# Twenty weight pieces converted early and parked in DRAM, four PSUM banks with a lag of three pairs, and a polynomial kept in PSUM

## The chip, the cores and the metric

The kernel runs on one core of a Trainium2 chip. The metric is the device time of one execution in microseconds (us); three runs of the kernel before the change gave 1054.34, 1056.89 and 1063.83 us, a median of 1056.89 us. The engines named below are PE (matrix multiply), DVE (vector), ACT (scalar functions), POOL (general purpose), SP (it only issues DMAs here), and PEld, the loading of weights into PE beside the multiplications.

## What is computed

Three stages follow one another on 4 batches of 576 tokens (2304 tokens in all).

```python
# stage 1: causal attention, 8 heads of width 64, plus a linear memory term
a = softmax(causal(q @ k.T / 8));  local = a @ v
mem_out = (phi(q) @ M_prev) / (phi(q) @ z_prev + 1e-6)     # phi(x) = elu(x) + 1
x = g * mem_out + (1 - g) * local                          # g = sigmoid(beta), per head
# stage 2, "first layer" (moe): 2304 x 512 -> 2048 -> 512
h = x @ moe_w_in;  x = (max(h, 0) + log1p(exp(-abs(h)))) @ moe_w_out
# stage 3, "second layer" (moe2): 2304 x 512 -> 2048 -> 512
h = x @ moe2_w_in
P = a0 + a1*h + a2*h**2 + a3*h**3;  Q = 1 + abs(b0)*abs(h) + abs(b1)*h**2
out = (P / (Q + 1e-6)) @ moe2_w_out
```

The four weight matrices arrive as 64-bit floats. The kernel has no 64-bit arithmetic, so each weight has to be put together as a 32-bit float from its two 32-bit halves by shifts and masks; below this is called converting.

## The kernel before, in words

**Pieces.** Each weight matrix is cut into 16 pieces of 128 partitions x 512 weights: 512 KB as it arrives, 256 KB once converted. `load_piece` issues the DMA. A piece is converted in one of two ways: `bits` takes three DVE instructions, `bits_abs` two on DVE, two on ACT and a multiplication on POOL. The tables `SIGN` and `SIGN2` say which piece takes which way. After that the pieces of moe_w_in, moe_w_out and moe2_w_in are scaled and split into a high and a low 16-bit float (`w_split`); the pieces of moe2_w_out become a high and a low 32-bit part (tiles w2oh and w2ol).

**First layer.** Tokens come in 12 groups (j = 0 to 11), each with 8 pairs of hidden rows, so that 96 pairs Q are worked off in order. `g1(Q)` multiplies a pair into PSUM bank 2 or 3 (`hf`), ACT takes Relu, Abs, Exp and Ln, DVE adds and subtracts, and the result goes into one of four buffers GH. `g2(Q)` multiplies GH into the accumulators in banks 0 and 1. PE gets g1(Q) and then g2(Q - LAG), with LAG = 2. Each of g1 and g2 is 24 matmuls with 160, 192 or 256 columns. Attention of later batches runs between the pairs and uses banks 4 to 7. The two first groups work in 32-bit floats and have fewer matmuls.

**Second layer.** The tokens are 6 blocks of 384 and the hidden rows 16 slices of 128, which gives 96 steps F. `h1(F)` is 12 matmuls of 384 columns into one of the banks 2 to 5 (`hp`, F modulo 4). ACT forms |h| and h squared, Ln and Exp (the reciprocal of Q); DVE forms the polynomial in six instructions; ACT rounds the result to its high part and POOL subtracts (tile `gr`). `h2_(F - 3)` is 9 matmuls of 512 columns into the accumulators, from `gr` and w2oh or w2ol. PE gets h1(F), then h2_(F - 3).

**What sets the order.** The program is first written down as a list of operations with keys. A planner, `Program.order`, then simulates the engines with a cost for each operation (`cost`) and a table of latencies, and on each engine takes the ready operation with the lowest key; `P.key` serves all engines and `P.pkey` serves PE. Some operations can go to one of two or three engines (`P.flex`), and the planner chooses. `P.emit` (L374, in the changed kernel L392) issues everything in this fixed order, so that nearly every row of the profile has that one line. All DMAs go through SP's queue, in order: a DMA that has to wait holds those behind it.

**The pieces of the second layer.** They have keys K0 = 1000 and up, after all of attention. They are loaded into two buffers (RAW2) in the space that attention has left, converted, and put in place: 16 pieces of moe2_w_in first (W2I), then 16 of moe2_w_out (W2O). The scale of moe2_w_in needs the largest weight of all 16 pieces, so that no split starts before the last of them is converted.

## Time and profile before

| | |
|---|---|
| median of three runs | 1056.89 us (1054.34 to 1063.83) |
| the profiled execution: time, span | 1058.07 us, 1056.1 us |
| mean granted clock of PE (share of full speed) | 0.976 |
| busy: PE, DVE, ACT, POOL | 984.7, 925.8, 837.8, 375.3 us |

The span runs from the first to the last instruction; the execution's own time is 2.0 us longer. Attention and the first layer fill the time to about 535 us; from there to about 650 us the rest of the first layer runs beside the conversion of the second layer's weights; then comes the second layer alone. The groups of rows below are cut from the profile's views: busy time by stretch, instructions in order of time, instructions grouped by form, and DMA issues. In a row of a view in order of time the bracket at the end holds the idle time before the instruction and what ended it.

### The profile page before, as it was taken

To read this page: it belongs to the slowest core of one execution; us is meant where nothing else is said; L and a number is where in the kernel's file an instruction comes from. 1 tells how busy PE (TensorE), PEld (TensorE's weight loads), DVE (VectorE), ACT (ScalarE), POOL (GpSimd) and SP (SyncE) were. 2 spreads that over 40 slices of the span, in tenths; PEclk is the share of its full clock that TensorE was granted. 3 is DMA by queue.
4 is the path that set the end of the run, shared out by engine and by line. 5 is a ranking of instruction groups with operands and counts; after the bars stand their busy time and mean duration, and the time that the engine had idled before them with its cause. 6 is when DMAs were issued, how large, how long until landed. Compare 5 with 4: busy or idle time off the path is not lost.

```text
span 1056.1 us, 22659 instructions
## 1 busy us (share of the span) xinstructions
PE 984.7 (93%) x8252; PEld 774.7 (73%) x8252; DVE 925.8 (88%) x2151; ACT 837.8 (79%) x1948; POOL 375.3 (36%) x427
## 2 busy tenths in 40 slices
PE   7779999999989999899898897998999999999998
PEld 6556777877778888788797896665766666666666
DVE  7999679988988997877768799999999999999896
ACT  5887978779889998777878777777778778687875
POOL 4323467852342422231033344333223223232222
PEclk9979999999999999989999999998999999999999
DMA  9986367577899977755755533010101000000000
GB/s 257 313 213 170 74 131 141 102 138 143 151 144 167 168 151 125 141 112 101 119 157 177 182 100 127 20 41 1 60 1 36 25 31 31 1 31 1 31 1 30
DMA packets 242975, 109.48 MB, mean 104 GB/s; under 512 B 218416, under 2 KB 224560, under 8 KB 242864
## 3 DMA queue, kind: packets, MB, share of 16 engines
q1 hardware_dynamic: 242864, 108.04, 45.6%
q8 instruction: 64, 1.05, 0.4%
q14 instruction: 47, 0.39, 0.1%
HBM read 59.25 MB, written 9.44 MB: 65 GB/s over the span
## 4 chain that ended last, share of the span: by engine, by line
PE 45%; DVE 14%; ACT 9%; DMA 6%; issue 3%; POOL 1%; SPq 1%; ACTq 0%; DVEq 0%; POOLq 0%
PE bank L374 45%; DVE arena L374 9%; ACT arena L374 5%; ACT bank L374 3%; DMA arena<-arena 2%; DMA arena<-in_moe_w_in_dram 2%; DVE bank L374 2%; DVE tiny L374 1%; SPq L374 1%; DMA arena<-in_moe_w_out_dram 0%; DMA arena<-x2d 0%; ACT a L374 0%; POOL arena L374 0%; DMA arena<-in_v_dram 0%; DVE a L374 0%
## 5 line engine op out<-in xcount | busy, mean ns | idle before, releaser
L374 PE MATMUL bank<-arena,w 128*128 128x160 f16 (+3 forms) x4288 | 422.4, 259 | 25.1 <-DVE arena L374 24.0
L374 PE MATMUL bank<-arena 128*128 128x384 f16 (+11 forms) x2852 | 356.6, 299 | 28.4 <-DVE arena L374 12.3
L374 ACT ACTIVATE arena<-bank,tiny 128x384 f32<-128x384 f32 (+8 forms) x538 | 300.0, 588 | 91.3 <-PE bank L374 81.2
L374 PEld LDWEIGHTS <-w 128*128 128x128 f16 x3840 | 298.9, 99 | 41.4 <-issue 32.4
L374 PEld LDWEIGHTS <-arena 128*128 128x128 f16 (+1 forms) x2464 | 159.9, 104 | 130.8 <-issue 58.1
L374 PE MATMUL bank<-w2oh,gr 128*128 128x512 f32 x576 | 206.2, 416 | 0.0
L374 POOL TENSOR_TENSOR gr<-arena,gr 128x384 fp32r<-128x384 f32 x94 | 102.0, 1085 | 262.2 <-ACT gr L374 240.5
L374 DVE SCALAR_TENSOR_TENSOR arena<-arena,tiny 128x384 f32<-128x384 f32 (+6 forms) x182 | 147.5, 823 | 11.2 <-ACT arena L374 9.5
L374 ACT ACTIVATE arena<-arena 128x384 f32<-128x384 f32 (+4 forms) x213 | 123.3, 580 | 13.4 <-DMA arena<-in_moe_w_in_dram 4.6
L374 PEld LDWEIGHTS bank<-w2oh,gr 128*128 128x128 f32 x576 | 109.5, 190 | 27.1 <-POOL gr L374 0.4
L374 DVE SCALAR_TENSOR_TENSOR arena<-arena 128x384 f32<-128x384 f32 (+3 forms) x168 | 117.8, 702 | 5.7 <-ACT arena L374 4.8
L374 POOL TENSOR_TENSOR arena<-arena 128x512 f32<-128x512 f32 (+6 forms) x68 | 66.2, 981 | 144.3 <-ACT arena L374 69.3
L374 ACT ACTIVATE bank<-bank,tiny 128x384 f32<-128x384 f32 (+4 forms) x192 | 102.5, 538 | 17.1 <-DVE tiny L374 16.1
L374 PE MATMUL bank<-w2ol,gr 128*128 128x512 f32 x288 | 114.3, 397 | 0.7 <-POOL w2ol L374 0.7
L374 ACT ACTIVATE bank<-bank 128x320 f32<-128x320 f32 (+2 forms) x208 | 103.5, 497 | 2.3
L374 ACT ACTIVATE arena<-bank 128x320 f16<-128x320 f32 (+5 forms) x148 | 72.1, 495 | 31.0 <-DVE bank L374 19.5
L374 PEld LDWEIGHTS bank<-arena,w 128*128 128x128 f32 x448 | 82.8, 190 | 14.0 <-issue 1.7
L374 DVE SCALAR_TENSOR_TENSOR arena<-bank,tiny,arena 128x384 f16<-128x384 f32 (+3 forms) x112 | 64.6, 592 | 19.1 <-ACT arena L374 17.2
L374 POOL TENSOR_SCALAR arena<-arena,tiny 128x640 f16<-128x640 f32 (+8 forms) x70 | 55.1, 793 | 61.8 <-DVE tiny L374 29.7
L374 ACT ACTIVATE arena<-arena,qe 128x384 f32<-128x384 f32 x96 | 58.9, 613 | 20.5 <-DVE arena L374 20.0
L374 DVE CUSTOM_DVE_ANT_0 bank<-bank,mask,tiny 128x384 f32<-128x384 f32 (+4 forms) x112 | 67.0, 609 | 5.8 <-PE bank L374 3.1
L374 DVE SCALAR_TENSOR_TENSOR arena<-arena,bb 128x384 f32<-128x384 f32 x96 | 67.0, 698 | 3.1 <-ACT arena L374 3.1
(108 smaller groups left out, 1115.2 us busy)
## 6 DMA issues: line engine op xcount, KB each, us to landing
arena<-in_moe_w_out_dram SPq DMA_DIRECT2D x32, 512.0 KB, 3.9
arena<-in_moe_w_in_dram SPq DMA_DIRECT2D x24, 512.0 KB, 4.9
arena<-in_k_dram SPq DMA_DIRECT2D x44, 128.0 KB, 3.6
arena<-in_v_dram SPq DMA_DIRECT2D x44, 128.0 KB, 2.9
arena<-arena SPq DMA_DIRECT2D x32, 160.0 KB, 3.0
arena<-x2d SPq DMA_DIRECT2D x6, 768.0 KB, 4.2
out_dram<-arena SPq DMA_DIRECT2D x18, 256.0 KB, 2.1
w<-in_moe_w_in_dram SPq DMA_DIRECT2D x8, 512.0 KB, 9.1
```

What stands on the lines that cost most here:

```text
L374: fn(**{k: (v.fn() if isinstance(v, Lazy) else v) for k, v in kw.items()})
```

## The change

- **Early pieces.** After pass 3 (the pass with all tokens of batch 3) `w2_early` takes all 16 pieces of moe2_w_in and 4 of moe2_w_out. It has keys from 2000 up, behind everything else. It loads each piece into the upper part of XA or XF, converts it into tile a1, and writes the 256 KB to a DRAM buffer `w2d`. Two of three pieces take the way of three DVE instructions (`SIGN3`). Behind attention the 20 pieces are then read from `w2d` to where they were converted to before.
- **Banks and lag.** LAG goes from 2 to 3, and pairs from Q = 80 on use banks 2 to 5 in turn for `hf`.
- **Polynomial in PSUM.** In `h1` two DVE instructions write their result back into the bank `hp` (before: into SBUF buffer l1), and a third reads it from there. The bank is thus in use up to the last of the six DVE instructions; before it was free after the third (the row that names `aa`).
- **Planner.** It now keeps a bank from being planned for two engines at once (`held`), and counts a pointer operand named `scale` in DVE's cost. The order of the whole program is made anew with this.

```diff
--- before.py
+++ after.py
@@ -22,7 +22,9 @@
 NT = B * S
 TB2 = 384
 NPAIR = DF // 256
-LAG = 2
+LAG = 3
+
+QLATE = 80
 PORT = 0.8
 EARLY = lambda load, u, consts, batch: (
     (lambda: load(u[0], 0, 1), lambda: load(u[1], 0, 1)),
...
@@ -48,6 +50,11 @@
 SIGN = ((1, 0), (0,))
 SIGN2 = ((1,), (0, 0, 1))
 LO_POOL = False
+
+NST = (16, 4)
+EARLY2 = {3: (0, 20)}
+KEY_ST = 2000
+SIGN3 = (0, 0, 1)
 BACKLOG = 4000.0
 NRAW = 6
 NGH = 4
...
@@ -138,7 +145,7 @@
         if name == "reciprocal":
             return 67 + 6.2 * n
         one = name in ("tensor_scalar", "tensor_copy", "memset") and not psum
-        aps = sum(is_ap(kw.get(k)) for k in ("scalar", "scalar1", "scalar2"))
+        aps = sum(is_ap(kw.get(k)) for k in ("scalar", "scalar1", "scalar2", "scale"))
         return (77 if name == "tensor_tensor_reduce" else 67) + (0.52 if one else 1.042) * n + 62 * aps
     if eng == "ACT":
         more = is_ap(kw.get("scale")) + is_ap(kw.get("bias")) + ("accum_out" in kw)
...
@@ -229,6 +236,9 @@
 
     def _deps(self, op, rd, wr):
         preds = set()
+        for v in rd + wr:
+            if is_psum(v):
+                op.banks.add(v.tensor.name)
         for v in rd:
             self._touch(span(v), op, False, preds)
         for v in wr:
...
@@ -288,6 +298,8 @@
         port = {"DVE": 0.0, "POOL": 0.0}
 
         now = dict.fromkeys(engines, 0.0)
+
+        held = {}
 
         def release(o):
             o.cand = {"BULK"} if o.bulk and "SP" in o.alts else set(o.alts)
...
@@ -326,6 +338,10 @@
                 continue
             k, i = heapq.heappop(ready[e])
             o = self.ops[i]
+            t = max((x + LATENCY[f][e] for b in o.banks for f, x in held.get(b, {}).items() if f != e), default=0.0)
+            if t > s:
+                heapq.heappush(wait[e], (t, k, i))
+                continue
             if len(o.cand) > 1:
                 mine = s + o.alts[e][0] * o.bias[e]
                 other = None
...
@@ -351,6 +367,8 @@
                 port[e] = s + dur
             o.dur = dur
             free[e] = end = s + dur
+            for b in o.banks:
+                held.setdefault(b, {})[e] = end
             if e == "SP":
                 free["BULK"] = end
                 dma_free = max(dma_free, s + min(dur, 650) + 625) + o.dma
...
@@ -412,6 +430,7 @@
     psum = ctx.enter_context(tc.tile_pool(name="psum", bufs=1, space=bass.MemoryType.PSUM))
 
     x2d = dram.tile([NT // TB2, 128, 4, TB2], F32, name="x2d")
+    w2d = dram.tile([32, 128, 512], F32, name="w2d")
     bank = [psum.tile([128, 512], F32, name=f"bank{i}") for i in range(8)]
 
 
...
@@ -1126,7 +1145,7 @@
     def g1(Q):
         j, p = divmod(Q, NPAIR)
         g, b, t0, tb = blk_g[j]
-        hf = bank[2 + Q % 2][:, 0:2 * tb]
+        hf = bank[2 + Q % (2 if Q < QLATE else 4)][:, 0:2 * tb]
         hp = hf.rearrange("p (f t) -> p f t", f=2)
         r = vw(RR[Q % 2], (2 * tb,), F32)
         if j < NF32:
...
@@ -1315,6 +1334,25 @@
         for pc in range(16):
             w_split(w1_place(which, pc, False), w1_place(which, pc + 2, True), s, True)
 
+    def w2_early(i0, i1):
+
+        steps = [(0, pc) for pc in range(NST[0])] + [(1, pc) for pc in range(NST[1])]
+        for i in range(i0, i1):
+            which, pc = steps[i]
+            P.key = KEY_ST + i
+            o = (XA, XF)[i % 2] + 1280
+            r = vw(o, (512, 2), U32)
+            load_piece((w_in_ap, w_out_ap)[which]((w2i, w2o)[which], pc), r)
+            dst = a_t[1][:, i % 2 * 512:i % 2 * 512 + 512]
+            acc = None if which else wacc[:, 32 + pc:33 + pc]
+            if SIGN3[i % len(SIGN3)]:
+                bits_abs(r, dst, a_t[1][:, 1024:1280].bitcast(BF16), acc)
+            else:
+                bits(r, dst.bitcast(U32))
+                if which == 0:
+                    A.activation(out=vw(o, (512,), F32), in_=dst, func=AF.Abs, accum_out=acc)
+            SP.dma_start(out=w2d[which * 16 + pc], in_=dst)
+
     P.key = -180
     for o in RAW:
         G.memset(vw(o, (10, D), F32)[64:128], 0.0)
...
@@ -1367,6 +1405,8 @@
         if p.i == 1:
             P.key = 30
             G.memset(an4[:, 4, :, 64:128], 0.0)
+        if p.i in EARLY2:
+            w2_early(*EARLY2[p.i])
 
 
     at_[0] = A0
...
@@ -1391,6 +1431,11 @@
     w2_i = [vw(o, (2048,), F16) for o in W2I]
     for pc in range(16):
         P.key = K0 + pc
+        if pc < NST[0]:
+            P.bulk = True
+            SP.dma_start(out=w2_place(pc + 1, True), in_=w2d[pc])
+            P.bulk = False
+            continue
         r = vw(RAW2[pc % 2], (512, 2), U32)
         load_piece(w_in_ap(w2i, pc), r)
         dst = w2_place(pc + 1, True)
...
@@ -1405,6 +1450,11 @@
         w_split(w2_place(pc, False), w2_place(pc + 1, True), w2.s)
     for pc in range(16):
         P.key = K0 + 40 + pc
+        if pc < NST[1]:
+            P.bulk = True
+            SP.dma_start(out=vw(W2O[pc], (512,), F32), in_=w2d[16 + pc])
+            P.bulk = False
+            continue
         r = vw(RAW2[pc % 2], (512, 2), U32)
         load_piece(w_out_ap(w2o, pc), r)
         if SIGN2[1][pc % len(SIGN2[1])]:
...
@@ -1510,10 +1560,11 @@
         A.activation(out=r0, in_=qa, func=AF.Ln, bias=qe)
         A.activation(out=r0, in_=r0, func=AF.Exp, scale=-1.0)
         tt(l1, t1, hp, ALU.mult, "V")
-        stt(l1, l1, aa[:, 1:2], hp, ALU.add, ALU.mult)
-        stt(l1, l1, y.a0, r0, ALU.add, ALU.mult)
+
+        stt(hp, l1, aa[:, 1:2], hp, ALU.add, ALU.mult)
+        stt(hp, hp, y.a0, r0, ALU.add, ALU.mult)
         stt(qa, qa, qe, r0, ALU.add, ALU.mult)
-        stt(l1, qa, 2.0, l1, ALU.subtract, ALU.mult)
+        stt(l1, qa, 2.0, hp, ALU.subtract, ALU.mult)
         scopy(gr_ap(F, 0, 0, TB2), l1, None, "AV")
         tt(gr_ap(F, 1, 0, TB2), l1, gr_ap(F, 0, 0, TB2, F32), ALU.subtract)
 
```

**SP's queue around the end of attention.** Here `arena<-arena` with DMA_TRANSPOSE is attention's transposition of its scores, `in_moe_w_in` is the load of a weight piece, and `a_99` is the tile a1. Before:

```order
296 L374 DMA x2d<-arena 512x1x160
297 L374 DMA_TRANSPOSE arena<-arena 128x8x128
298 L374 DMA_TRANSPOSE arena<-arena 128x12x128
299 L374 DMA_TRANSPOSE arena<-arena 128x8x128
300 L374 DMA_TRANSPOSE arena<-arena 128x10x128
301 L374 DMA arena<-in_moe_w_in_dram 128x2x512
302 L374 DMA arena<-x2d 128x1536
303 L374 DMA arena<-in_moe_w_in_dram 128x2x512 x4
```

And in the changed kernel:

```order
292 L392 DMA_TRANSPOSE arena<-arena 128x6x128
293 L392 DMA w2d<-a_99 128x512
294 L392 DMA arena<-w2d 128x512
295 L392 DMA arena<-in_moe_w_in_dram 128x2x512
296 L392 DMA_TRANSPOSE arena<-arena 128x12x128
297 L392 DMA_TRANSPOSE arena<-arena 128x8x128
298 L392 DMA arena<-w2d 128x512
299 L392 DMA arena<-in_moe_w_in_dram 128x2x512
300 L392 DMA_TRANSPOSE arena<-arena 128x10x128
```

Writes of converted pieces, reads of them and loads of further pieces now stand between attention's transposes. On DVE, nine of the twenty early conversions stand ahead of the last softmax instruction of attention and eleven behind it.

**DVE in the second layer, ten to twenty steps after its start.** The six instructions of a step are those that name `tiny`, `qe`, `bb`, `aa` and the bank, and the one with `arena<-arena 128x384` alone; rows with 128x512 convert pieces of moe2_w_out. Before:

```order
1440 L374 TENSOR_TENSOR arena<-arena,bank_69 128x384
1441 L374 TENSOR_SCALAR arena<-arena 128x512
1442 L374 SCALAR_TENSOR_TENSOR arena<-arena,tiny 128x384
1443 L374 SCALAR_TENSOR_TENSOR arena<-arena,qe 128x384
1444 L374 SCALAR_TENSOR_TENSOR arena<-arena,bb 128x384
1445 L374 SCALAR_TENSOR_TENSOR arena<-arena 128x384
1446 L374 SCALAR_TENSOR_TENSOR arena<-arena,aa,bank_69 128x384
1447 L374 TENSOR_TENSOR arena<-arena,bank_70 128x384
1448 L374 SCALAR_TENSOR_TENSOR arena<-arena 128x512
```

And in the changed kernel:

```order
1457 L392 TENSOR_TENSOR arena<-arena,bank_70 128x384
1458 L392 SCALAR_TENSOR_TENSOR bank_70<-arena,aa,bank_70 128x384
1459 L392 SCALAR_TENSOR_TENSOR arena<-arena,qe 128x384
1460 L392 SCALAR_TENSOR_TENSOR bank_70<-bank_70,tiny,arena 128x384
1461 L392 SCALAR_TENSOR_TENSOR arena<-arena,bb 128x384
1462 L392 SCALAR_TENSOR_TENSOR arena<-arena,bank_70 128x384
1463 L392 TENSOR_TENSOR arena<-arena,bank_71 128x384
```

The conversions have gone from this place: in the changed order none stands behind the first step's polynomial, where before there were 17 such instructions. Three of the six instructions of a step now name the bank as output or as the only other input, and the step keeps it up to the row `arena<-arena,bank_70`.

## Rows read from the trace of the kernel before

**Rows 1.** The page: span, then busy time, share and instructions of each engine.

```profile
span 1056.1 us, 22659 instructions
PE 984.7 (93%) x8252; PEld 774.7 (73%) x8252; DVE 925.8 (88%) x2151; ACT 837.8 (79%) x1948; POOL 375.3 (36%) x427
```

**Rows 2.** The chain that ended last, in time order: start, duration, what.

```profile
734.85 315.69 PE bank L374 x1617
```

**Rows 3.** Busy time by stretch: length, busy time of each engine, clock, DMA share, GB/s.

```profile
515.00:536.00 21.00, 19.70 (x331) 18.27 (x329) 11.49 (x31) 15.84 (x41) 0.00 (x0) 1.00 0.66 111
...
536.00:600.00 64.00, 54.40 (x732) 52.68 (x730) 50.08 (x97) 53.12 (x132) 28.44 (x30) 0.97 0.60 188
600.00:650.00 50.00, 45.34 (x598) 42.45 (x597) 47.10 (x89) 35.02 (x77) 21.80 (x22) 1.00 0.32 103
650.00:735.00 85.00, 75.46 (x388) 50.72 (x385) 84.09 (x130) 63.66 (x123) 30.94 (x25) 0.94 0.11 35
735.00:1052.00 317.00, 317.00 (x1623) 218.40 (x1624) 292.07 (x533) 242.26 (x482) 92.03 (x89) 0.99 0.06 21
```

**Rows 4.** PE in order of time: start, duration, instructions; idle time before, releaser.

```profile
533.21 2.33 PE L374 MATMUL bank<-arena 128*64 128x128 f16 x62
...
551.65 3.48 PE L374 MATMUL bank<-arena,w 128*128 128x160 f16 x48 [0.47 <-DVE arena L374]
...
665.28 0.88 PE L374 MATMUL bank<-w2oh,gr 128*128 128x512 f32 x1
...
1052.05 0.40 PE L374 MATMUL bank<-w2oh,gr 128*128 128x512 f32 x1
```

**Rows 5.** Groups of instructions by form, 760 to 1040 us: count, busy, mean ns, idle.

```profile
L374 ACT ACTIVATE arena<-bank,tiny 128x384 f32<-128x384 f32 x207 | 119.0, 606 | 49.8 <-PE bank L374 48.1 <-DVE arena L374 0.4
L374 PE MATMUL bank<-arena 128*128 128x384 f16 x827 | 145.5, 327 | 0.0
...
L374 DVE SCALAR_TENSOR_TENSOR arena<-arena,tiny 128x384 f32<-128x384 f32 x70 | 57.6, 823 | 8.2 <-ACT arena L374 7.6
...
L374 DVE SCALAR_TENSOR_TENSOR arena<-arena,aa,bank 128x384 f32<-128x384 f32 x70 | 42.8, 612 | 5.3 <-ACT arena L374 3.7
L374 DVE SCALAR_TENSOR_TENSOR arena<-arena 128x384 f32<-128x384 f32 x70 | 39.4, 563 | 0.2
...
L374 DVE TENSOR_TENSOR arena<-arena,bank 128x384 f32<-128x384 f32 x70 | 38.3, 547 | 3.5 <-ACT arena L374 3.1
```

**Rows 6.** DVE in order of time.

```profile
523.95 0.62 DVE L374 SCALAR_TENSOR_TENSOR arena<-bank,tiny,arena 128x384 f16<-128x384 f32 x1 [1.45 <-ACT arena L374]
...
650.60 1.62 DVE L374 SCALAR_TENSOR_TENSOR arena<-arena,bb 128x384 f32<-128x384 f32 x1
...
660.05 0.60 DVE L374 SCALAR_TENSOR_TENSOR arena<-arena,tiny 128x384 f32<-128x384 f32 x1
660.58 0.54 DVE L374 SCALAR_TENSOR_TENSOR arena<-arena 128x384 f32<-128x384 f32 x1
```

**Rows 7.** Groups of instructions by form, 536 to 640 us: the conversions on DVE.

```profile
L374 DVE SCALAR_TENSOR_TENSOR arena<-arena 128x512 uint32<-128x512 uint32 x28 | 24.3, 867 | 0.3
L374 DVE TENSOR_SCALAR arena<-arena 128x512 uint32<-128x512 uint32 x22 | 14.3, 649 | 5.4 <-DMA arena<-in_moe_w_in_dram 5.4
```

**Rows 8.** Busy time by stretch, in attention.

```profile
240.00:440.00 200.00, 188.76 (x2307) 163.56 (x2304) 175.63 (x533) 179.66 (x449) 61.19 (x92) 0.99 0.84 153
440.00:536.00 96.00, 85.99 (x1234) 78.28 (x1233) 69.39 (x208) 71.78 (x187) 18.23 (x28) 0.95 0.62 108
```

**Rows 9.** PE's waits, 440 to 536 us: total, times, longest.

```profile
PE bank L374 <- DVE arena L374: 7.0, 7, 2.2
```

**Rows 10.** DMA issues: count, size of one, median us from issue to landing.

```profile
arena<-in_moe_w_in_dram SPq DMA_DIRECT2D x24, 512.0 KB, 4.9
...
out_dram<-arena SPq DMA_DIRECT2D x18, 256.0 KB, 2.1
```

**Rows 11.** Waits of SP's queue over the whole span: total, times, longest.

```profile
SPq L374 <- DVE arena L374: 266.3, 70, 21.8
```

More of the change, by code (lines that the diff above doesn't have):

```diff
@@ L158 @@
 class Op:
-    __slots__ = ("bulk", "alts", "cand", "eng", "key", "pkey", "succ", "npred", "ready", "start", "idx", "done", "dma", "bias", "port", "dur")
+    __slots__ = ("bulk", "alts", "cand", "eng", "key", "pkey", "succ", "npred", "ready", "start", "idx", "done", "dma", "bias", "port", "dur", "banks")
 class Program:
@@ L245, in _new @@
         op.alts, op.eng, op.key, op.pkey = {}, None, self.key, self.pkey
-        op.bulk, op.bias, op.port = self.bulk, self.bias, set()
+        op.bulk, op.bias, op.port, op.banks = self.bulk, self.bias, set(), set()
         op.succ, op.npred, op.ready, op.start, op.idx, op.done, op.dma = set(), 0, 0.0, 0.0, len(self.ops), False, 0
```

## The prediction

> **What bounds the kernel now.** The page comes first: PE is busy for 984.7 of 1056.1 us, more than any other engine, so that at most some 71 us of its idle time can be won [rows 1]. The chain of waits says where: from 734.85 us on it is one piece of PE work of 315.69 us [rows 2], and the busy times by stretch agree, since from 735 to 1052 us PE has no idle time at all [rows 3]. Nothing that makes another engine faster there can shorten it; only its beginning can move. So the question is how much PE work is left at a given time, and how much of the time before 735 us PE loses.
>
> I price PE's work at full speed. A pair of the first layer with 160 columns takes 3.48 us for its 48 matmuls [rows 4]. A step F of the second layer takes 4.06 us: in the 280 us from 760 to 1040 us there are 827 matmuls of h1, 12 to a step, so 68.9 steps [rows 5]. Attention's last matmuls end at 533.2 + 2.3 = 535.5 us [rows 4]; in PE's order 1,308 matmuls of the first layer stand behind them, which is 27.25 pairs. What is left is 27.25 x 3.48 = 94.8 and 96 x 4.06 = 389.8, together 484.6 us. The last matmul ends at 1052.05 + 0.40 [rows 4], so the stretch lasts 516.9 us and 32.3 us are lost. Of these PE visibly waits for 64.0 - 54.4 = 9.6, 50.0 - 45.3 = 4.7 and 85.0 - 75.5 = 9.5 us in the three stretches up to 735 us; the other 8.5 go with granted clocks of 0.97 and 0.94 there [rows 3].
>
> The last of the three stretches is held by DVE: it is busy for 84.1 of 85 us, with the polynomial and what is left of the conversions, and PE follows it [rows 3]. In the two before, DVE is busy for 50.1 of 64 and 47.1 of 50 us.
>
> **The change, part by part.**
>
> *The conversions that leave.* In the changed order none of them stands behind the first step of the second layer; before there were 17 instructions, 6 of the short and 11 of the long kind, 6 x 0.65 + 11 x 0.87 = 13.5 us of DVE [rows 7]. That empties the stretch from 650 to 735 us of what PE followed there.
>
> *The conversions that stay behind attention.* Only nine of twenty go ahead of attention's end. In DVE's order 200 instructions stand from attention's last normalisation to the first step's polynomial; in the changed order 197, with 61 conversion instructions instead of 58. So the work on DVE in this stretch is the same, and a gain here can only come from its idle time. Before, the stretch ran from 523.95 to 650.60 us [rows 6], 115.1 us beyond attention's last matmul. DVE idles in it for up to 21.0 - 11.5 = 9.5, 13.9 and 2.9 us, 26.3 in all [rows 3], partly for want of loaded pieces [rows 7]. The early pieces are ready to fill that, since their buffers are free before attention ends. Between all of it and none I take half, 13 us, as they share SP's queue and two buffers with 4.9 us to a load [rows 10]. The polynomial then starts 102 us behind attention's end.
>
> *Where PE stands by then.* The changed order leaves 25.75 pairs behind attention, 89.6 us, and so puts 1.5 pairs, 5.2 us, ahead of its end. Lag and banks: PE's waits in this stretch are mostly of the kind of the 0.47 us ahead of the pair in [rows 4], for the DVE instruction that frees bank 2 or 3. The last 16 pairs get four banks, so that three other pairs' work, some 10 us, lies between two uses of a bank; I leave 5 us of waits for the rest. PE has done the pairs after about 95 us and the first h1 steps after some 10 more, and then waits for the first polynomial. Before, the first h2 ran 665.3 - 650.6 = 14.7 us behind the polynomial's start [rows 4, 6], with conversions in between. Without them I take 9.5: six instructions of 0.55 to 0.6 us for this step and as many for its neighbour [rows 6], then rounding and subtraction. [...] Sum: 493.8 us, where 516.9 - 5.2 = 511.7 would be no change: **17.9 us won.**
>
> *Attention.* Nine pieces at, on average, 2.1 us of DVE (2.4 for two of three, 1.5 for the third [rows 7]) are 19 us put into attention, in the 296 us of which DVE idles for 24.4 + 26.6 = 51 [rows 8]. The bounds are 0 (all of it in gaps) and +19 us (all of it ahead of something PE needs). I take 2.7 us, near the lower end, as there is two and a half times as much idle time as work to put in it. Against it stands the lag: seven of PE's waits in the last 96 us are for DVE, 7.0 us [rows 9], and a third pair under way gives PE 1.7 us more to do in each; I take half, 3.5 us. Together -0.8.
>
> *The polynomial in PSUM.* The instruction with `tiny` takes 823 ns on average, but 0.60 us where POOL doesn't run beside it [rows 5, 6]; those that have a bank among their operands take 612 and 547 ns on average [rows 5]. So DVE saves about 0.2 us a step, 20 us in 96, and nothing of it shows, since PE sets the pace from there on. [...]
>
> *DRAM and SP.* The 20 loads are the same; 20 writes and 20 reads of 256 KB are new, about 2.1 us each [rows 10]. I cost them at nothing: the first reader of a read-back piece is the split, far behind it. Without that cover the cost is that of a rival below.
>
> Sum: 17.9 + 0.8 = 18.7 us off the profiled 1058.07, so 1039.4; the profiled execution lies 0.1% above the median of 1056.89. **I forecast 1040 us**, 1.6% below the median. Differences under about 1% can't be told from no change here.
>
> **Rivals.**
>
> *DVE's gaps are not filled.* Two buffers and one queue feed the early pieces as they fed the late ones; if all 26 us of idle time stay, the polynomial starts 115 us behind attention's end, PE waits for it, and only the leaving conversions count: 1040 + 13 = 1053 us. For it speaks that DVE waited for loads of just these pieces [rows 7]; against it that twice as many buffers now take them. Chance 0.17.
>
> *Attention gets shorter.* A new order of everything, with the third pair in flight, might take all of PE's 7.0 us of waits and half of the 21.2 us that PE idles in 296 us [rows 8, 9], while DVE's gaps behind it go too: 1040 - 13 = 1027 us. Chance 0.15.
>
> *SP's queue makes it slower.* A write of a piece has to wait for its conversion, which has the lowest key of all, and attention's transposes stand behind it in the queue; PE needs those. SP already waits 266.3 us for DVE [rows 11]. If each of nine pieces passes its 2.1 us of DVE and the 2.1 us of its write on to PE, 38 us are lost: 1078 us. It decides from 3.1 us a piece (28 us in all), where the time is 1% above the median. Against it: SP's queue runs ahead, and DVE idles 17% of these stretches [rows 8]. Chance 0.08.
>
> *The bank is held too long.* A step keeps its bank through h1 (2.0), two of ACT's passes (0.6 each [rows 5]), Ln and Exp and six DVE instructions shared with a neighbour, some 10 us of the 4 x 4.06 = 16.2 in which the bank comes round. If it takes 17 us, each step costs 0.2 us more: 1040 + 19 = 1059. It needs 6 us more than I count. Chance 0.05.
>
> The forecast keeps 0.55. Its own range is 1033 to 1048, from DVE's idle time filled wholly or by a quarter and attention's cost between 0 and +5. For eight in ten I go on to the second rival's 1027 with a few us to spare, and up to the first and the last: **1024 to 1060 us**. Faster by over 1% (below 1046.3): 0.50 of the forecast and the second rival, 0.65. Slower by over 1% (above 1067.5): 0.08 and what lies above 1060 of the rest, 0.10. Within: 0.25.
>
> **What would show it.** Right: PE's idle time from 735 us on stays zero and a step keeps 4.06 us; no 128x512 conversions on DVE behind the first polynomial; the first h2 runs about 110 us behind attention's last matmul instead of 129.7; attention's last matmul at 535 to 545 us. The saving on DVE shows as the `tiny` instruction near 0.6 us. Wrong: attention's end beyond 555 us with PE waiting for transposes (SP's queue), DVE idle time of over 20 us between attention and the polynomial (the first rival), or PE waits inside the second layer released by the last DVE instruction of a step (the bank).

## The result, and the profile after

The changed kernel takes **1022.71 us** (median of four runs, 1017.00 to 1030.09), the kernel before 1057.6 beside it on the same chip. The ratio is 0.969 with a 95% interval of 0.965 to 0.973: 3.1% faster, where 1.6% was forecast. The time lies 1.3 us below the range. The profiled execution took 1025.81 us. All numbers below, medians and ratios apart, come from one execution of each kernel. Executions of one kernel differ by some us (here by 13), so a difference of under 5 us in one term is not read as an effect.

The page, as in [rows 1]:

```profile
span 1023.9 us, 22739 instructions
PE 974.1 (95%) x8252; PEld 766.7 (75%) x8252; DVE 909.6 (89%) x2164; ACT 824.9 (81%) x1914; POOL 380.1 (37%) x438
```

PE's idle time fell from 71.4 to 49.8 us, and its busy time from 984.7 to 974.1 us for the same 8252 matmuls, with a mean granted clock of 0.982 instead of 0.976. The chain of waits ends as before in one piece of PE work. It now starts at 637.22 us, not at 734.85 [rows 2]. Behind it, from 987 us on, the chain runs through the last steps' work on ACT, DVE and POOL, since PE waits 0.16 us for the last subtraction; that wait is all that it costs:

```profile
637.22 349.98 PE bank L392 x1814
...
1018.28 1.90 PE bank L392 x7
```

Busy time by stretch (length; PE, PEld, DVE, ACT, POOL; granted clock, DMA share, GB/s), against [rows 3, 8]:

```profile
240.00:440.00 200.00, 188.48 (x2322) 164.46 (x2321) 178.93 (x546) 176.68 (x447) 68.85 (x104) 0.98 0.90 167
440.00:536.00 96.00, 89.76 (x1328) 81.24 (x1326) 80.10 (x230) 81.77 (x218) 25.53 (x36) 0.98 1.01 211
```

```profile
536.00:600.00 64.00, 59.48 (x839) 58.29 (x837) 61.00 (x125) 48.66 (x116) 23.90 (x27) 1.00 0.69 233
600.00:650.00 50.00, 46.61 (x480) 39.15 (x478) 46.22 (x82) 42.58 (x93) 25.97 (x22) 1.00 0.23 72
```

```profile
639.00:735.00 96.00, 96.00 (x499) 66.00 (x497) 90.15 (x167) 73.26 (x143) 29.61 (x29) 1.00 0.05 17
735.00:1020.00 285.00, 284.84 (x1470) 194.67 (x1468) 259.79 (x473) 217.65 (x422) 81.96 (x82) 1.00 0.05 18
```

From 639 us on PE has no idle time worth naming, so the stretch that DVE held before, 650 to 735 us, is gone. In the 64 us behind attention DVE is busy for 61.0 us instead of 50.1, and PE for 59.5 instead of 54.4. The granted clock is 1.00 in all four stretches behind attention, where it was 0.97 and 0.94 in two of them [rows 3].

PE in order of time, to be laid beside [rows 4]: attention's last matmuls, the last wait before the second layer runs free, the first h2, and the last matmul.

```profile
530.72 2.09 PE L392 MATMUL bank<-arena 128*64 128x128 f16 x62
...
637.22 2.11 PE L392 MATMUL bank<-arena 128*128 128x384 f16 x12 [1.57 <-DVE arena L392]
639.03 0.53 PE L392 MATMUL bank<-w2oh,gr 128*128 128x512 f32 x1
...
1019.78 0.39 PE L392 MATMUL bank<-w2oh,gr 128*128 128x512 f32 x1
```

Attention ends at 532.8 us (before 535.5), and the first h2 follows 106.2 us later (before 129.7, forecast 111.5).

**Three sums.** The orders leave different amounts of work behind attention, so I compare kernels by three sums that take this out, with the prices of the prediction. A is the end of attention's last matmul plus 3.48 us for each pair still to do. M is the stretch from there to the first h2, less those pairs and less 2.03 us for each h1 step done in it. T is the stretch from the first h2 to the last matmul plus 2.03 us for those h1 steps; 96 x 4.06 = 389.8 would be its floor. A + M + T is the end of the last matmul.

| | A (attention) | M (middle) | T (tail) | sum | A less start |
|---|---|---|---|---|---|
| before | 630.3 | 20.7 | 401.4 | 1052.4 | 534.8 |
| forecast | 629.5 | 11.9 | 392.3 | 1033.7 | 534.0 |
| changed | 622.4 | 6.4 | 391.3 | 1020.2 | 521.1 |

For the changed kernel, A is 532.8 + 25.75 x 3.48, M is 106.2 - 89.6 - 5 x 2.03, and T is 1020.2 - 639.0 + 5 x 2.03. For the forecast, A is 630.3 - 0.8, M is 111.5 - 89.6 - 10 and T is 389.8 + 2.5: the first h2 was to begin 102 + 9.5 = 111.5 us behind attention's end with five h1 steps done, and 2.5 us of the 493.8 stood for a lower clock.

**The start.** A also holds the first 100 us, and these differ from profile to profile while the work in them is the same. PE's first 500 matmuls are the same work in all kernels of this document, the first 363 in the same order; yet the 363rd begins at 72.3 us in the quickest profile and at 81.2 in the slowest, and the 501st at 95.5 us in the kernel before, at 101.3 in the changed one, and anywhere from 94.3 to 105.0 in the others. I call this time, the beginning of the 501st matmul, the start. In three profiles the granted clock of PE goes with it: between 30 and 100 us, where it stands at 0.50 in some parts (58 to 70 us in the kernel before, 66 to 78 in the changed one) and at 1.00 in others (72 to 100 and 80 to 100 us), it is on average 0.88 in the kernel before, 0.80 in the changed kernel and 0.90 in that with 24 early pieces, which starts at 95.1 us:

```profile
30.00:100.00 70.00, 59.36 (x341) 42.12 (x341) 66.87 (x182) 56.68 (x165) 20.70 (x18) 0.88 0.91 243
```

```profile
30.00:100.00 70.00, 58.19 (x322) 39.82 (x321) 60.69 (x177) 52.90 (x156) 21.99 (x15) 0.80 0.88 237
```

```profile
30.00:100.00 70.00, 58.33 (x349) 41.33 (x349) 67.34 (x196) 56.72 (x168) 24.26 (x18) 0.90 0.91 245
```

Four of the kernels below (changed, polynomial in SBUF, 24 early pieces, lag 3 with two banks) run the same instructions in the same order on PE, DVE, ACT and POOL up to attention's end. Their A ranges from 616.5 to 622.4, the changed kernel's being the largest, but A less the start only from 521.0 to 524.1. So effects in attention are read from A less the start. Each kernel has one profile, and that executions of one kernel differ in this way is not shown; it would fit that of the six profiles that start at 101 us or later four lie 3 to 5.5 us above the median of their kernel, and of the eight others none more than 1.7.

### The profile page after: what moved, and what is told of

It is laid out like the page before. It is cut to its first block, busy times and chain, and to the rows that moved or that the text cites. A ratio compares the mean times of both kernels' runs of the same rounds, so it can differ in the third digit from the quotient of the medians.

```text
span 1023.9 us, 22739 instructions
## 1 busy us (share of the span) xinstructions
PE 974.1 (95%) x8252; PEld 766.7 (75%) x8252; DVE 909.6 (89%) x2164; ACT 824.9 (81%) x1914; POOL 380.1 (37%) x438
## 4 chain that ended last, share of the span: by engine, by line
PE 38%; DVE 11%; DMA 9%; ACT 7%; issue 3%; SPq 1%; POOL 1%; POOLq 0%; DVEq 0%; ACTq 0%
PE bank L392 38%; DVE arena L392 5%; ACT arena L392 4%; DMA arena<-arena 3%; ACT bank L392 3%; DVE bank L392 2%; DVE tiny L392 1%; DMA arena<-a 1%; DMA arena<-in_moe_w_out_dram 1%; DVE a L392 1%; SPq L392 1%; DMA arena<-in_moe_w_in_dram 1%; DMA arena<-in_q_dram 1%; POOL arena L392 1%; DMA arena<-x2d 1%
## 5 line engine op out<-in xcount | busy, mean ns | idle before, releaser
L392 ACT ACTIVATE arena<-bank,tiny 128x384 f32<-128x384 f32 (+8 forms) x536 | 290.8, 593 | 71.3 <-PE bank L392 65.5
L392 PEld LDWEIGHTS <-w 128*128 128x128 f16 x3840 | 294.0, 98 | 25.9 <-issue 15.3
L392 DVE SCALAR_TENSOR_TENSOR bank<-bank,tiny,arena 128x384 f32<-128x384 f32 (+2 forms) x176 | 106.9, 608 | 25.7 <-ACT arena L392 11.8
L392 ACT ACTIVATE arena<-arena 128x384 f32<-128x384 f32 (+4 forms) x177 | 100.6, 569 | 12.8 <-POOL arena L392 4.0
L392 ACT ACTIVATE bank<-bank,tiny 128x384 f32<-128x384 f32 (+5 forms) x192 | 103.1, 545 | 5.7 <-DVE tiny L392 5.3
L392 ACT ACTIVATE arena<-bank 128x320 f16<-128x320 f32 (+5 forms) x150 | 73.2, 497 | 33.2 <-PE bank L392 18.8
L392 POOL TENSOR_SCALAR arena<-arena,tiny 128x640 f16<-128x640 f32 (+9 forms) x81 | 61.9, 772 | 77.5 <-PE bank L392 28.1
L392 ACT ACTIVATE arena<-arena,qe 128x384 f32<-128x384 f32 x96 | 59.0, 615 | 21.1 <-DVE arena L392 18.7
L392 DVE SCALAR_TENSOR_TENSOR arena<-arena,qe 128x384 f32<-128x384 f32 x96 | 74.1, 772 | 0.2 <-ACT arena L392 0.2
L392 POOL TENSOR_TENSOR arena<-arena 128x192 f32<-128x192 f32 (+7 forms) x55 | 52.9, 970 | 56.8 <-DVE arena L392 20.6
L392 DVE SCALAR_TENSOR_TENSOR arena<-bank,tiny,arena 128x384 f16<-128x384 f32 (+4 forms) x112 | 64.0, 592 | 9.3 <-ACT arena L392 7.9
L392 DVE SCALAR_TENSOR_TENSOR arena<-arena,tiny 128x384 f16<-128x384 f32 (+5 forms) x84 | 69.5, 837 | 0.9 <-POOL arena L392 0.8
```

What stands on the lines that cost most here:

```text
L392: fn(**{k: (v.fn() if isinstance(v, Lazy) else v) for k, v in kw.items()})
```

## The experiments

My theory: three parts work together. The early pieces empty the tail and give DVE something to do behind attention; lag and banks let PE do more of the first layer in attention; the polynomial in PSUM is worth nothing. The four kernels below the changed one leave one part out of it, the next three are the kernel before with one part alone, and the last five vary one size. Ratios are to the kernel before, run beside each.

| kernel | median us | ratio (95% interval) | A | A less start | M | T |
|---|---|---|---|---|---|---|
| changed | 1022.7 | 0.969 (0.965 to 0.973) | 622.4 | 521.1 | 6.4 | 391.3 |
| without early pieces | 1040.6 | 0.985 (0.981 to 0.989) | 614.5 | 513.2 | 8.1 | 417.0 |
| lag 2, two banks | 1044.2 | 0.988 (0.984 to 0.991) | 634.0 | 531.9 | 13.3 | 391.7 |
| planner as before | 1041.5 | 0.984 (0.979 to 0.988) | 623.7 | 525.9 | 8.3 | 394.9 |
| polynomial in SBUF | 1022.6 | 0.967 (0.963 to 0.971) | 617.0 | 521.0 | 4.6 | 394.1 |
| early pieces alone | 1045.2 | 0.988 (0.984 to 0.992) | 635.8 | 530.8 | 12.2 | 391.1 |
| lag and banks alone | 1046.4 | 0.993 (0.989 to 0.996) | 623.1 | 519.8 | 10.8 | 412.2 |
| planner alone | 1051.5 | 0.995 (0.991 to 0.999) | 619.2 | 524.2 | 23.3 | 404.1 |
| lag 3, two banks | 1028.6 | 0.972 (0.969 to 0.976) | 618.4 | 524.1 | 14.2 | 391.8 |
| each piece written twice | 1025.4 | 0.972 (0.968 to 0.976) | 618.2 | 522.0 | 7.6 | 392.6 |
| 24 early pieces | 1020.8 | 0.967 (0.965 to 0.969) | 616.5 | 521.4 | 7.0 | 391.4 |
| 9 early pieces | 1027.0 | 0.974 (0.970 to 0.977) | 615.8 | 521.4 | 9.5 | 391.1 |
| early pieces the other way | 1026.1 | 0.971 (0.968 to 0.975) | 619.1 | 517.8 | 13.4 | 391.4 |

**Without early pieces.**

```diff
-NST = (16, 4)
-EARLY2 = {3: (0, 20)}
+NST = (0, 0)
+EARLY2 = {}
```

> The changed kernel without early pieces: all 32 pieces of the second layer are loaded and converted behind attention as before; lag 3, four banks, the polynomial in PSUM and the planner's bank rule stay. In its order 24 pairs stand behind attention, 48 conversion instructions on DVE between the last softmax and the first polynomial and 27 behind it. Theory 1 (the early pieces fill DVE's idle time behind attention and empty the second layer's start of conversions): about 1042 us (+18 to +24 over 1022.7), the first h2 some 125 us behind attention's last matmul or PE waiting again in the 60 us behind it. Theory 2 (banks and lag won most): 1030 us or less. Theory 3 (the new order of attention won most): 1030 us or less, with attention's end at about 533 us or earlier.

Measured: 1040.6 us. Attention gets better by 7.9 us (both profiles start at 101.3 us) and the tail worse by 25.7. DVE's groups of 128x512 instructions behind the first h2 (632.9 to 735 us; count, busy us, mean ns, idle) show what stands in it now:

```profile
L392 DVE SCALAR_TENSOR_TENSOR arena<-arena 128x512 uint32<-128x512 uint32 x17 | 16.6, 979 | 0.1
L392 DVE TENSOR_SCALAR arena<-arena 128x512 uint32<-128x512 uint32 x9 | 5.2, 588 | 0.0
L392 DVE SCALAR_TENSOR_TENSOR arena<-arena,tiny 128x512 f16<-128x512 f32 x5 | 4.3, 864 | 0.0
```

That is 26.1 us of conversions and splits, against 25.7 us that the tail got longer. Lag and banks had brought the second layer forward, and the conversions slid behind its start. That the two numbers are so close is in part chance: of the 25.7 us PE waits for 17.8 in this tail, 9.0 of them for DVE and 8.6 for POOL and ACT, which make w2ol and w2oh from the same pieces, and the granted clock is 0.95 up to 735 us. PE's waits, 632.9 to 1039.7 us:

```profile
PE bank L392 <- DVE arena L392: 9.0, 7, 2.2
PE bank L392 <- POOL w2ol L392: 5.9, 6, 1.4
PE bank L392 <- ACT w2oh L392: 2.7, 2, 1.5
```

**Lag 2 and two banks.**

```diff
-LAG = 3
+LAG = 2
-QLATE = 80
+QLATE = 10000
```

> The changed kernel with LAG = 2 and banks 2 and 3 alone for all pairs; early pieces, polynomial in PSUM and the planner's bank rule stay. Theory 1 (early pieces): 1023 to 1028 us, as PE's waits in the pairs lie beside DVE's work on conversions. Theory 2 (banks and lag): 1032 us or more, with PE waits of 10 us or more for DVE between attention's end and the first h2, as before, and 5 us more of them inside attention.

Measured: 1044.2 us; A is 11.6 us worse (10.8 from the start), M 6.9, the tail untouched. Just ahead of the second layer PE waits once for DVE:

```profile
653.97 4.00 PE L392 MATMUL bank<-arena 128*128 128x384 f16 x12 [5.64 <-DVE arena L392]
```

**The planner as before.**

```diff
-                held.setdefault(b, {})[e] = end
+                pass
```

(and the cost without `scale`)

> The changed kernel planned without the rule that keeps a bank for one engine at a time and without the extra cost of a pointer scale; the operations are the same. In its order only 20 pairs stand behind attention instead of 25.75. Theory 3 (the planner's rule gave attention its 8 us): 1030 to 1035 us, with more PE waits inside attention. Theories 1 and 2: within 4 us of 1022.7.

Measured: 1041.5 us in the median. Its profiled execution took 1032.3 us, at the fast end of 1032.3 to 1044.0, and its three sums add up to 6.7 us more than those of the changed kernel (3.6 of them in T; from the start it is 10.2, with 4.8 in A), where the medians lie 18.8 us apart. Where the rest goes stays open.

**The polynomial in SBUF.**

```diff
-        stt(hp, l1, aa[:, 1:2], hp, ALU.add, ALU.mult)
-        stt(hp, hp, y.a0, r0, ALU.add, ALU.mult)
+        stt(l1, l1, aa[:, 1:2], hp, ALU.add, ALU.mult)
+        stt(l1, l1, y.a0, r0, ALU.add, ALU.mult)
...
-        stt(l1, qa, 2.0, hp, ALU.subtract, ALU.mult)
+        stt(l1, qa, 2.0, l1, ALU.subtract, ALU.mult)
```

> The changed kernel with the polynomial's two results back in SBUF. If PE sets the pace of the second layer, as the forecast has it: 1021 to 1026 us, 4.06 us a step, no PE idle time from 700 us on. If writing the bank saves time on the path: 1030 us or more. If holding the bank costs: 1018 us or less.

Measured: 1022.6 us, no difference. The two instructions that change places, 760 to 1000 us, first in this kernel, then in the changed one:

```profile
L392 DVE SCALAR_TENSOR_TENSOR arena<-arena,tiny 128x384 f32<-128x384 f32 x60 | 57.8, 963 | 10.6 <-ACT arena L392 10.5
L392 DVE SCALAR_TENSOR_TENSOR arena<-arena,qe 128x384 f32<-128x384 f32 x60 | 38.7, 645 | 0.2
```

```profile
L392 DVE SCALAR_TENSOR_TENSOR arena<-arena,qe 128x384 f32<-128x384 f32 x59 | 46.5, 788 | 0.0
...
L392 DVE SCALAR_TENSOR_TENSOR bank<-bank,tiny,arena 128x384 f32<-128x384 f32 x59 | 36.5, 619 | 9.7 <-ACT arena L392 8.9
```

The `tiny` instruction gives up 344 ns, and the one with `qe` takes 143 of them back. Over its six instructions DVE saves 0.16 us a step (3.95 us against 3.79), and PE doesn't wait for it.

**One part alone.** Each of these is the changed kernel with all other parts undone; shown is what then differs from the kernel before. The early pieces alone:

```diff
+NST = (16, 4)
+EARLY2 = {3: (0, 20)}
```

> The kernel before with the early pieces alone (lag 2, two banks, polynomial in SBUF, no bank rule in the planner). If the early pieces are worth their 18 us by themselves: 1038 to 1042 us, with the time behind the first h2 falling from 387 to about 381 us and attention no longer than before. If they need the other parts (the pairs wait for banks whatever DVE does): 1046 to 1056 us, with the waits of PE for DVE inside and behind attention as before (some 15 us each).

Lag and banks alone:

```diff
-LAG = 2
+LAG = 3
+QLATE = 80
```

> The kernel before with lag 3 and four banks from pair 80 alone. In its order 25 conversion instructions stand behind the first polynomial, before 17. If the parts add up: 1036 to 1040 us, 20 us won. If what the lag wins ahead of the first h2 is given back behind it, as in the run without early pieces (where 26 conversions and 5 splits, 26 us of DVE, made the rest 26 us longer): 1046 to 1056 us, with the first h2 10 us or more earlier than at 665 us and over 395 us behind it.

The planner's two rules alone:

```diff
+                held.setdefault(b, {})[e] = end
```

(and the cost with `scale`)

> The kernel before, planned with the bank rule and the cost of a pointer scale, no other part. 24.25 pairs stand behind attention, 20 conversions behind the first polynomial. If the rule shortens attention by itself: 1042 to 1048 us, with less PE waiting up to attention's end. If it only suits the other parts: 1053 to 1062 us.

Measured: 1.2, 0.75 and 0.5% faster, while leaving one of them out costs 1.6, 1.8 and 1.4% of the time before. So lag and banks, and the planner's rules, win about 1% more beside the other parts than alone, just beyond the intervals; for the early pieces, and between the sum of the three (2.5%) and the 3.1% of the whole change, the difference lies within them. The early pieces alone empty the tail (T 391.1) and take 8.5 us off M. Their A is 5.5 us larger than before, but that is no cost of theirs: this profile starts 9.5 us later, no early piece is converted before 309 us, and from the start A is 4.0 us smaller. Lag and banks alone win 15.0 us in A from the start and 9.9 in M and give 10.8 back in the tail; the planner alone wins 10.6 us in A from the start and gives 5.3 back behind it. In the kernel with lag and banks alone PE has no work for long stretches from 680 to 735 us, while DVE works off what slid behind (same columns as above):

```profile
680.00:735.00 55.00, 39.45 (x179) 24.89 (x177) 51.02 (x79) 38.18 (x76) 24.63 (x20) 0.91 0.17 58
```

**Lag 3 with two banks.**

```diff
-QLATE = 80
+QLATE = 10000
```

> The changed kernel with lag 3, but banks 2 and 3 alone for all pairs. If it is the lag that took PE's waits away: 1022 to 1027 us. If it is the four banks of the last 16 pairs: PE waits 5 to 10 us more behind attention's end, 1028 to 1034 us, and attention's end as in the changed kernel.

Measured: 1028.6 us. The third pair in flight carries most of this part: from lag 2 to lag 3 with two banks the ratio goes from 0.988 to 0.972, beyond both intervals; four banks bring 0.003 more, within them. What they change is visible in one wait, at the same place as with lag 2; in the changed kernel it is 1.57 us:

```profile
639.25 4.00 PE L392 MATMUL bank<-arena 128*128 128x384 f16 x12 [5.97 <-DVE arena L392]
```

**Each early piece written twice.**

```diff
-    w2d = dram.tile([32, 128, 512], F32, name="w2d")
+    w2d = dram.tile([64, 128, 512], F32, name="w2d")
...
+            SP.dma_start(out=w2d[32 + which * 16 + pc], in_=dst)
```

> The changed kernel with each of the 20 early pieces written twice to DRAM (20 more writes of 256 KB on SP's queue, nine of them within attention; nobody reads the second copy). My theory: SP's queue and the DMA engines have room for them, and what attention pays for the early pieces is DVE's and PE's order, not the queue: within 3 us of the changed kernel (1020 to 1026 us), attention's last matmul at 531 to 536 us, about 106 us from there to the first h2. Rival, SP's queue: each write that waits for its conversion holds the transposes behind it; the second copy leaves at once behind the first, so it adds only the 2 us of its own transfer for each piece: nine in attention, some 18 us, attention's last matmul at 545 us or later, 1035 to 1045 us, with PE waiting for DMAs.

Measured: 1025.4 us, attention's last matmul at 529.5 us. So SP's queue has room for 20 more writes. The DMA issues (count, KB each, median us to landing) show them, and PE's waits from 240 us to attention's end are 7.9 us for DMAs, 3.3 more than in the changed kernel:

```profile
w2d<-a SPq DMA_DIRECT2D x40, 256.0 KB, 3.4
```

```profile
PE bank L392 <- DMA arena<-arena: 7.9, 7, 2.5
```

**Twenty-four early pieces.**

```diff
-NST = (16, 4)
-EARLY2 = {3: (0, 20)}
+NST = (16, 8)
+EARLY2 = {3: (0, 24)}
```

> The changed kernel with four more pieces of moe2_w_out taken early (24 instead of 20). In its order as many pairs are left behind attention as with 20 (25.75), and no conversion stands behind the first polynomial, as with 20. My theory: once the tail behind the first polynomial is empty of conversions, there is nothing more to win from early pieces: 1018 to 1026 us, the tail at the same 391 us of PE work. Rival, early pieces each cost attention 0.3 to 0.4 us (from +5.5 and +7.9 us for 20): 1 to 2 us slower, 1024 to 1025. Rival, fewer conversions between attention and the first polynomial bring the first h2 forward: 5 us faster, 1017.

Measured: 1020.8 us (1020.72 to 1022.65). The tail is the same, and so is A less the start (521.4). The interval of its ratio overlaps that of the changed kernel, so no version here is shown to beat it.

**Nine early pieces.**

```diff
-NST = (16, 4)
-EARLY2 = {3: (0, 20)}
+NST = (9, 0)
+EARLY2 = {3: (0, 9)}
```

> The changed kernel with nine early pieces of moe2_w_in and none of moe2_w_out (9 instead of 20). In its order 15 conversion instructions stand behind the first polynomial (27 without any early piece, 0 with 20), and 24.5 pairs are left behind attention. My theory: the tail costs what DVE spends on the conversions that stand in it; 15 instructions at 0.6 to 0.9 us, 9 to 13 us, less 3 to 4 us that attention gets back: 1027 to 1033 us, the tail at 400 to 404 us. Rival, it is the pieces of moe2_w_in alone that count, since their splits can't start before the scale is known: then nine pieces bring little, about 1036 to 1041 us as with none.

Measured: 1027.0 us in the median, and there my theory is wrong in its working. The median lies at the lower edge of what I gave, but the tail of the profiled execution (1022.65 us, the fastest of four) is at its floor. Fifteen conversion instructions stand behind the first polynomial, eight of them behind the first h2 (637.6 to 690 us):

```profile
L392 DVE SCALAR_TENSOR_TENSOR arena<-arena 128x512 uint32<-128x512 uint32 x5 | 6.0, 1202 | 0.0
L392 DVE TENSOR_SCALAR arena<-arena 128x512 uint32<-128x512 uint32 x3 | 2.7, 895 | 0.0
```

PE doesn't wait for them:

```profile
640.00:680.00 40.00, 40.00 (x211) 27.52 (x209) 39.48 (x68) 31.23 (x63) 15.71 (x15) 1.00 0.05 14
```

The first polynomial starts 17.9 us ahead of the first h2 here, 8.2 in the changed kernel: DVE comes into the tail with a head start, and 8.7 us of conversions fit into it. In the kernels that lose in T the same rows hold 13.2 us (before), 16.0 (planner alone), 18.0 (lag and banks alone) and 26.1 us (without early pieces), for losses of 10.1, 12.8, 20.9 and 25.7 us. It may be that what stands behind the first h2 costs about its own time only from the point where DVE's head start is used up. That is not shown: it is read from five profiles and not tried, and in the kernel before the polynomial starts 14.7 us ahead of the first h2, not much less than here, and 13.2 us of conversions still cost 10.1.

A less the start is 521.4 here, as with 20 and 24 pieces: the pieces that stand in attention cost it as much when no others follow them.

**The early pieces converted the other way** (two DVE instructions, two on ACT, one on POOL for each of them):

```diff
-SIGN3 = (0, 0, 1)
+SIGN3 = (1,)
```

> The changed kernel with all 20 early pieces converted by two DVE, two ACT instructions and a multiplication on POOL, instead of two of three by three DVE instructions: 0.87 us less DVE for each of 13 pieces, and more for ACT and POOL. In its order 25.25 pairs are left behind attention (25.75 before), and nothing stands behind the first polynomial. My theory: DVE's work for the early pieces is what costs attention its 5 to 8 us; about five of those nine pieces within attention take less of it, 4 to 5 us in all, so attention's last matmul comes 2 to 4 us earlier for the same pairs: 1016 to 1021 us. Rival, it's the order as a whole and not DVE's load: no difference, 1021 to 1025. [...]

Measured: 1026.1 us (1022.8 to 1029.6), the same within the intervals. A is 3.3 us better, the way my theory had it but no more than profiles of one order differ, and M is 7.0 worse, with PE waiting 5.0 us in three waits for small POOL results behind attention:

```profile
PE bank L392 <- POOL tiny L392: 5.0, 3, 2.1
```

## Why the prediction came out as it did

The direction was right, and so was the mechanism behind attention's end. Two sizes were too small, that of attention by far, and part of attention's gain came from a place that the prediction did not look at. Of the 32.2 us between the last matmuls 18.7 were forecast.

*The tail (forecast -9.1, measured -10.1): right.* No conversion stands behind the first h2, a step still takes 4.06 us, and PE doesn't wait. Leaving the early pieces out brings the loss back, and the early pieces alone are enough to take it away. Before, T lay 11.6 us above its floor, and 5.9 of them were waits of PE; the rest goes with the granted clock of 0.94 in 650 to 735 us [rows 3], which is 1.00 now. No run shows the 2.5 us that the forecast kept for a lower clock behind the first h2: T is 1.5 us above its floor in the changed kernel and 1.3 with the early pieces alone.

*DVE's gaps behind attention (forecast -8.8 in M, measured -14.3): too small.* I took half of 26.3 us. From the last 384-column normalisation to the first polynomial DVE took 126.7 us before, 104.2 of them busy; now it takes 109.0 from the end of that instruction on, 98.4 busy. So idle time fell by 12 us, close to the half, but the work also got some 5 us shorter (the instruction left out is 0.6), which I had excluded ("the work on DVE in this stretch is the same"). Busy time by stretch, before and changed (DVE is the third of the engines):

```profile
523.95:650.60 126.65, 111.19 (x1519) 106.12 (x1517) 104.24 (x201) 96.62 (x231) 50.62 (x52) 0.99 0.50 148
```

```profile
521.85:630.85 109.00, 101.72 (x1440) 98.38 (x1438) 98.37 (x194) 86.79 (x207) 45.99 (x45) 1.00 0.62 198
```

The groups of conversions in that stretch, before first, then changed:

```profile
L374 DVE SCALAR_TENSOR_TENSOR arena<-arena 128x512 uint32<-128x512 uint32 x32 | 28.0, 876 | 0.4
...
L374 DVE TENSOR_SCALAR arena<-arena 128x512 uint32<-128x512 uint32 x26 | 16.0, 614 | 10.3 <-DMA arena<-in_moe_w_in_dram 8.2 <-DMA arena<-in_moe_w_out_dram 2.1
```

```profile
L392 DVE SCALAR_TENSOR_TENSOR arena<-arena 128x512 uint32<-128x512 uint32 x20 | 16.3, 814 | 0.0
...
L392 DVE SCALAR_TENSOR_TENSOR a<-arena,a 128x512 uint32<-128x512 uint32 x17 | 13.1, 773 | 0.2
...
L392 DVE TENSOR_SCALAR arena<-arena 128x512 uint32<-128x512 uint32 x12 | 6.5, 546 | 3.7 <-DMA arena<-in_moe_w_out_dram 3.7
...
L392 DVE TENSOR_SCALAR a<-arena 128x512 uint32<-128x512 uint32 x10 | 6.0, 598 | 0.4 <-DMA w2d<-a 0.4
```

58 conversion instructions became 59, their time 44.0 us became 41.9, and the idle time ahead of the short kind (TENSOR_SCALAR), for DMAs, fell from 10.3 to 4.1 us. The rest of the shorter work lies mainly in shorter splits (1.5 us) and in four instructions fewer for the pairs (2.2). The polynomial started 98.0 us behind attention's end (forecast 102), and h2 ran 8.2 us behind it (forecast 9.5).

*Attention (forecast -0.8, measured -7.9, and -13.7 from the start): the step that was mis-sized most.* Attention's last matmul ended at 532.8 us, ahead of the 535 to 545 that the prediction named. The second half of the term, -3.5 us for the lag, was far too low: from the start it is 15.0 us alone and 10.8 in the full set. I had priced only PE's seven waits for DVE in the last 96 us; in the same stretch they are now 4.6 us, and PE is busy for 3.8 us more in it [rows 8, 9]. PE's waits for DVE, 440 to 536 us (total, times, longest):

```profile
PE bank L392 <- DVE arena L392: 4.6, 5, 1.5
```

About half of the gain lies earlier. From the 501st to the 2001st matmul, the same work in both kernels and ahead of the first conversion of an early piece, PE needs 199.5 us instead of 206.0, at the same granted clock (before, then changed):

```profile
95.60:301.60 206.00, 196.03 (x1501) 157.50 (x1500) 179.14 (x497) 175.49 (x429) 109.22 (x132) 0.98 0.66 123
```

```profile
101.30:300.80 199.50, 193.10 (x1501) 157.03 (x1500) 177.52 (x496) 173.39 (x425) 114.07 (x135) 0.98 0.66 126
```

This goes with the lag: the same stretch takes 206.1 to 209.0 us in the four kernels with lag 2, and 199.5 to 203.3 in the ten with lag 3.

The first half, +2.7 us for the early pieces, was too low in the full set (7.9 us; the other three profiles of the same order say 7.8 to 10.9, all against one profile without early pieces), and too high for the early pieces alone, where no cost shows. Their work is the 19 us that I counted, but by luck: up to attention's end 31 conversion instructions of early pieces run on DVE, some eleven pieces, at 0.61 us each, where I had nine pieces at 2.1 us. Two fifths of it are passed on in the full set, not a seventh:

```profile
L392 DVE SCALAR_TENSOR_TENSOR a<-arena,a 128x512 uint32<-128x512 uint32 x19 | 13.8, 725 | 0.2
...
L392 DVE TENSOR_SCALAR a<-arena 128x512 uint32<-128x512 uint32 x12 | 5.1, 423 | 2.2 <-DMA arena<-in_moe_w_in_dram 1.8 <-DMA w2d<-a 0.4
```

And I gave the planner's two rules no price. Alone they win 10.6 us in A from the start; in the full set 4.8 show, too few to tell from nothing. This is where the forecast of a new order is weakest: the sums say how much PE work stood ahead of attention's end, not which of the planner's choices put it there, and no run tells that apart.

*The polynomial (forecast: DVE 0.2 us a step, nothing of it visible): right.* In the same order but for this part a step's DVE work is 0.16 us shorter with the bank (3.79 us against 3.95). What I had missed is that part of the time moves on to the next instruction (143 of 344 ns). Against the kernel before, DVE saves only about 0.07 us a step.

*DRAM and SP (forecast nothing): right in the sum, not in every step.* Writes took 3.3 us and reads 4.4 us from issue to landing (medians) instead of the 2.1 that I had taken, and twice as many writes change nothing that shows. But the last piece's write and read-back stand in the chain of waits that leads to the first h2, and ACT begins the piece's split right behind them; what that costs no run tells:

```profile
606.73 5.70 DMA w2d<-a
612.45 2.66 DMA arena<-w2d
```

Of the rivals, the second (attention gets shorter, 1027 us) came nearest, with DVE's gaps going too, as it said; but it looked for the gain from 240 us on, and about half lies ahead of 301 us. The gaps were filled, SP's queue did not hold attention, and PE did not wait in the second layer for a bank that a step had kept too long. So the outcome is the forecast's behind attention, and nearer to the second rival's in attention.

## What to carry to other kernels

Where one engine sets the end without a gap, look for the work of another engine that stands in front of its start, and move that into an earlier stretch with idle time; price the stretch it goes to as well, since here up to two fifths of it was passed on there. Parts that shorten different stretches need not add up: bringing the last stage forward is worth little until what it would collide with is out of the way, so undo each part and try each alone. Before a difference between two profiles is put down to an edit, compare them at a point that both reach by the same work: here they were up to 9 us apart while they still ran the same instructions in the same order. When a planner's rules change, allow for as much as the largest priced term, in either direction.

## What the runs showed of the hardware

DVE's instruction with `qe`, which has its operands in SBUF, is longer where POOL's runs beside it; the one with `aa` and a bank is not. In the changed kernel, 760 to 1000 us, the first takes 0.61 us in each of 28 cases without POOL, and 0.97 on average in the 29 in which POOL runs for at least 0.2 us of it; the second takes 0.61 to 0.62 in all of its 12 cases without and 47 with POOL. DVE in order of time in the changed kernel, then POOL in the same microseconds:

```profile
801.62 0.61 DVE L392 SCALAR_TENSOR_TENSOR arena<-arena,qe 128x384 f32<-128x384 f32 x1
...
803.73 0.62 DVE L392 SCALAR_TENSOR_TENSOR bank<-arena,aa,bank 128x384 f32<-128x384 f32 x1
804.29 1.07 DVE L392 SCALAR_TENSOR_TENSOR arena<-arena,qe 128x384 f32<-128x384 f32 x1
```

```profile
803.92 1.02 POOL L392 TENSOR_TENSOR gr<-arena,gr 128x384 fp32r<-128x384 f32 x1 [3.39 <-ACT gr L392]
```

The instruction with two SBUF operands takes 0.61 us alone and 1.07 us beside POOL; it ends 0.4 us after POOL's. The one with a bank operand runs into POOL's and takes 0.62 us all the same. The means above add that where one of two neighbours was freed, 143 ns of its 344 went to the other.
